# Gradients and inner rows turned by DMA instead of TensorE, PSUM halves kept, large loads held: a four-layer forward and backward

## The chip, the core and the metric

The kernel runs on one core of a Trainium2 chip. Its time is the device time of one execution in microseconds (us); of several executions the median is taken. A profile is a record of one execution of its own. The core has five instruction queues: TensorE (PE; its weight loads are shown as PEld), VectorE (DVE), ScalarE (ACT), GpSimd (POOL) and SyncE (SP). Here SP computes nothing: it issues DMA transfers, in order, and an issue that must wait holds up all that stand behind it. POOL issues some transfers too.

## What is computed

The reference is a forward pass of four residual layers over x [2048, 512], A, B, A, B, and the gradients of its output with respect to x and to five weights. In short:

```
A(x): q, k, v = (x @ wqkv) in 32 heads of 16;  pq, pk = phi(q), phi(k)
      kv = sum_s pk v;  z = sum_s pk;  o = (pq kv) / (pq z + 1e-6);  return o @ wo
B(x): h = sigmoid(x @ w_gate) * (x @ w_up);  return h @ w_down      # inner width 1376
x = x + A(LN(x)); x = x + B(LN(x)); x = x + A(LN(x)); x = x + B(LN(x))
outputs: x, and the gradients for A_x, wqkv, wo, w_gate, w_up, w_down from grad_out
```

Both A layers share their weights, and both B layers theirs, so a weight's gradient is a sum over two layers. Matmul operands are bf16 and sums are f32.

## The kernel before

The 2048 rows stand in 16 tiles of 128 rows, in 4 blocks of 4 tiles (512 rows). The width of 512 is 4 chunks of 128, and the inner width of 1376 is 11 chunks (`NFC`). Layers are called 0 (A), 1 (B), 2 (A), 3 (B). The residual x, later the gradient, stays in SBUF as 16 f32 tiles `k.xs`. The stages in order of time, by the profile of before:

- 0 to 70 us: layer 0 forward, first half (`AFwd.first`: layer norm, keys, sums over all rows).
- 70 to 300 us: its second half (`second`) woven into layer 1 (`b_fwd`, `glu`), then layer 2, whose second half runs beside the start of layer 3.
- 300 to 519 us: layer 3 forward and backward at once (`b_both`, L709). A block makes, for each of 11 chunks, the gate and the up products and the gradient of the inner rows (`g_ps`, `u_ps`, `dhh_ps`), the inner rows `hh` and two gradient factors `dd`. After the second chunk (fc 1) of the next block come `down` (the output rows) and `dh_b` (L796, the gradient to the layer norm, closed by `ln_bwd`, L857).
- 519 to 634 us: layer 2 backward: `a_bwd1` (L970) and `a_bwd2` (L1044).
- 634 to 759 us: layer 1 backward (`b_bwd`, L877).
- 759 to 866 us: layer 0 backward, by the same two functions.
- 866 to 1115 us: the weights' gradients from saved rows (`dw_cols` L1205, `dw_rows` L1227), which need both layers' saved operands with rows on the partitions (`set_t`, `rows_t`).

One gradient is not left to the end. `Fill` (L211) computes layer 3's part of the gradient of w_down as 11 x 16 = 176 single matmuls (`fill_ps`, L236), and `k.fill.step(n)` puts n of them in where TensorE would wait otherwise. Their operand is `hh` of layer 3 with rows on the partitions. Before, `store_hh` (L658) writes `hh` to DRAM as it stands (inner index on the partitions, `sv_hhT`), for layer 3 from POOL's queue, and `Fill.load` (L221) reads it back with a transposing DMA of 16 tiles for each inner chunk (`hf_t`, L224).

`a_grads` (L940) makes a block's gradient ready for the attention's backward: ACT rounds `k.xs` to bf16 (`ga_t`, L947), TensorE turns it in 128x128 pieces (`T_ps`, L951), and ACT copies the turned pieces out of PSUM (`gaT_t`, L953). It is called for block 0 within the stage before, and for the other blocks in halves inside `a_bwd1`. `b_grads` (L957) does the same for layer 1 with a DMA in place of TensorE (L964).

`a_bwd1` loops over 4 blocks and 4 chunks: `dq_ps` (4 matmuls on `gaT_t` and `MT_l`), an ACT copy `dq_sb`, a product `u_t` with the loaded `qp_l`, and `soft` two chunks later (`t_ps`, then DVE, and POOL on the loaded `dqT_t`); a block ends with 16 matmuls into `CT_ps` that need `ga_t` and the loaded `qn_l`. `a_bwd2` first forms small products (`dkvT`, `Wp`, `Nv`), and then for each block `dpk_ps` (16 matmuls on the loaded `haT_l`, drained by DVE into `dkT_t`, L1075, with a factor from the loaded `pkT_l`), and three groups of 16 matmuls into `dh_ps` (L1062, and twice L1123), closed by `ln_bwd`.

The order on each engine is set by a list scheduler that follows the order of the program text and its priorities; `after` and `held` (L184, L191) add an edge by hand, `held` one that a transfer must wait for. Tiles come from pools with a fixed number of buffers: a new tile waits for the last user of the buffer it takes. PSUM has 8 banks. Before, the forward pass takes all 8 from one pool (L342, tag "bank"), and the backward pass opens two new pools of 4 (L814, L815, tags "bank" and "dwbank"). The buffers that the steps name are `h_t` (4; holds `h_t`, `gn_t`, `ga_t`, `qn_l`, `ha_l`), `hT_t` (4), `sh` (2), `set_t` (6) and `hh` (14).

Of the kernel before, what the change touches and what calls it, by code (L numbers as in the profile page):

```python
# [51 lines left out]
class K:  # L52
    pass
# [3 lines left out]
def kernel(  # L57
# [42 lines left out]
    for l in range(4):  # L100
# [11 lines left out]
        else:  # L112
            d["hhT"] = dram.tile([F, S], BF16, name=f"sv_hhT{l}")
            d["ddT"] = dram.tile([2, F, S], BF16, name=f"sv_ddT{l}")
            if l == 3:
                d["g"] = k.g_in
                d["wd"] = dram.tile([F, D], F32, name="sv_wd3")
                d["ddN"] = dram.tile([NBLK, len(SETS), P, 2, NB, D], BF16, name="sv_ddN3")
            else:
                d["g"] = dram.tile([S, D], BF16, name=f"sv_g{l}")  # L120
                d["sd"] = dram.tile([NBLK, NFC, P, 2 * SB], BF16, name=f"sv_sd{l}")
# [4 lines left out]
    k.gns, k.gTs, k.nats = {}, {}, []  # L126

    k.wb = ExitStack()
    forward(k)
# [81 lines left out]
class Fill:  # L211


    def __init__(self, k):
        self.k, self.sv = k, k.sv[3]
        self.g = [k.p_set.tile([P, NB, D], BF16, name="gf_t", tag="set_t") for _ in range(NBLK)]
        for b in range(NBLK):
            k.nc.sync.dma_start(out=self.g[b][:], in_=by_tile(k.g_in, b * NB, NB))
        self.todo = self.run()

    def load(self, fc):  # L221
        t = self.k.p_set.tile([P, NST, P], BF16, name="hf_t", tag="set_t")
        w = min(P, F - fc * P)
        self.k.nc.sync.dma_start_transpose(out=t[:, :, 0:w], in_=self.sv["hhT"][fc * P:fc * P + w, :])  # L224
        return t, w

    def run(self):
        k, nc = self.k, self.k.nc
        ahead = self.load(0)
        for fc in range(NFC):  # L230
            t, w = ahead
            ps = k.ps.tile([P, D], F32, name="fill_ps", tag="bank")
            for st in range(NST):
                if st == 3 and fc + 1 < NFC:
                    ahead = self.load(fc + 1)
                nc.tensor.matmul(ps[0:w, :], lhsT=t[:, st, 0:w], rhs=self.g[st // NB][:, st % NB, :],  # L236
# [12 lines left out]
class LN:  # L249
# [12 lines left out]
    def one(self, st):  # L262
# [5 lines left out]
        if l == 0:  # L268
# [13 lines left out]
            if j % 2 == 0:  # L282
                self.tp = k.ps.tile([P, 2 * NDC, P], BF16, name="T_ps", tag="bank")
# [31 lines left out]
    def turn(self, j):  # L315

        k, nc = self.k, self.k.nc
        tp = k.ps.tile([P, 2 * NDC, P], BF16, name="T_ps", tag="bank")
# [16 lines left out]
def forward(k):  # L335
    nc, tc = k.nc, k.tc
    with ExitStack() as ctx:
# [4 lines left out]
        k.ps = pool("ps_fwd", 8, space=PSUM)  # L342
# [89 lines left out]
class AFwd:  # L432
# [6 lines left out]
    def keys(self, st):  # L439
# [6 lines left out]
        k_ps = k.ps.tile([P, D], F32, name="k_ps", tag="bank")  # L446
# [11 lines left out]
    def first(self, done):  # L458

        k, nc, l, ln = self.k, self.k.nc, self.l, self.ln  # L460
        E_ps = [k.ps.tile([P, D], F32, name="E_ps", tag="bank") for _ in range(NDC)]
        z_ps = k.ps.tile([P, NDC], F32, name="z_ps", tag="bank")
# [30 lines left out]
        self.E_ps, self.z_ps = E_ps, z_ps  # L493

    def query(self, b, d2):
# [5 lines left out]
        for i in range(2):  # L501
            dc = 2 * d2 + i
            q_ps = k.ps.tile([P, SB], F32, name="q_ps", tag="bank")
# [7 lines left out]
    def den(self, b, _=0):  # L511

        k, nc = self.k, self.k.nc
        d_ps = k.ps.tile([P, P], F32, name="den_ps", tag="bank")
# [10 lines left out]
    def share(self, b, d2):  # L525
# [3 lines left out]
        for i in range(2):  # L529
            ps = k.ps.tile([P, SB], F32, name="rd_ps", tag="bank")  # L530
# [19 lines left out]
    def out(self, b, j):  # L550
        k, nxt = self.k, self.nxt
        y_ps = k.ps.tile([P, D], F32, name="y_ps", tag="bank")
# [5 lines left out]
    def products(self, E, kvT):  # L558
# [3 lines left out]
        k2_ps = k.ps.tile([P, NDC, P], F32, name="kv_ps", tag="bank")  # L562
# [5 lines left out]
        for jc in range(NDC):  # L568
            m_ps = k.ps.tile([P, D], F32, name="MT_ps", tag="bank")
# [6 lines left out]
    def second(self, nxt):  # L576
# [19 lines left out]
        kv_ps = k.ps.tile([P, NDC, P], F32, name="kvT_ps", tag="bank")  # L596
# [6 lines left out]
        for c in range(NDC):  # L603
            m_ps = k.ps.tile([P, D], F32, name="M_ps", tag="bank")
# [30 lines left out]
def glu(k, hT, fc, fused=False):  # L635

    nc = k.nc
    g_ps = k.ps.tile([P, SB], F32, name="g_ps", tag="bank")
    mm4(k, g_ps[:], lambda c: k.wg[:, c, FC0[fc]:FC0[fc] + P], lambda c: hT[:, :, c, :])
    u_ps = k.ps.tile([P, SB], F32, name="u_ps", tag="bank")  # L640
# [22 lines left out]
def b_fwd(k, l, ln, nxt):  # L663
# [9 lines left out]
    def down(b):  # L673
        ys = [k.ps.tile([P, D], F32, name="y_ps", tag="bank") for _ in range(NB)]
# [34 lines left out]
def b_both(k, l, ln, ctx):  # L709
# [4 lines left out]
    k.n_t, k.fused = 2, lambda st: True  # L714

    def down(b):
        for j in range(NB):
            st = b * NB + j
            y_ps = k.ps.tile([P, D], F32, name="y_ps", tag="bank")
# [15 lines left out]
    for b in range(NBLK):  # L735
        ln.need(b * NB + NB - 1)
        hhs[b], dds[b] = [], []
        if b == 1:
            k.p_ln, k.p_o, k.p_nat = pool("ln3", 2), pool("o3", 2), pool("nat", 2)
        for fc in range(NFC):  # L740
            hh, dd = glu(k, ln.hT[b], fc)
            ps = k.ps.tile([P, SB], F32, name="dhh_ps", tag="bank")
# [8 lines left out]
            store_hh(k, sv, b, fc, hh, k.st)  # L751
# [7 lines left out]
            if b == NBLK - 1 and fc == 5:  # L759
                k.early = a_grads(k, 0)  # L760
# [4 lines left out]
    dh_b(k, l, b, dds[b], ln.h[b], gns[b])  # L765
    flush_nat(k)
# [17 lines left out]

def flush_nat(k):
# [10 lines left out]
def dh_b(k, l, b, dds, h, up=None):  # L796
    for j in range(NB):
        st = b * NB + j
        dh_ps = k.ps.tile([P, D], F32, name="dh_ps", tag="bank")
# [10 lines left out]
def backward(k):  # L810
    nc, tc = k.nc, k.tc
    with ExitStack() as ctx:
        pool = lambda name, bufs, **kw: ctx.enter_context(tc.tile_pool(name=name, bufs=bufs, **kw))
        k.ps = pool("ps_bwd", 4, space=PSUM)  # L814
        k.ps2 = pool("ps_dw", 4, space=PSUM)  # L815
# [17 lines left out]
        h3, h1 = (load_all(k, sv[l]["h"], k.p_all, "all") for l in (3, 1))  # L833
# [43 lines left out]
def b_bwd(k, l):  # L877
    nc, sv = k.nc, k.sv[l]
    with ExitStack() as ctx:
# [8 lines left out]
        def back(b, fc, dd):  # L888

            if fc == 0:  # L890
                acc[b] = [k.ps2.tile([P, D], F32, name="dh_ps", tag="dwbank") for _ in range(NB)]
# [10 lines left out]
        gTs[0] = k.early  # L902
        for b in range(NBLK):
            if b == NBLK - 1:
                k.early = a_grads(k, 0)
            for f0, nf in FGRP:
# [3 lines left out]
                for fc in range(f0, f0 + nf):  # L910
                    i = fc - f0
                    ps = k.ps.tile([P, SB], F32, name="dhh_ps", tag="bank")
# [12 lines left out]
                    if fc == 3 and b + 1 < NBLK:  # L925
                        grads(b + 1)
        while late:
# [12 lines left out]
def a_grads(k, b, half=None):  # L940
    nc = k.nc
    if half in (None, 0):
        k.ga = (k.p_h.tile([P, NB, D], BF16, name="ga_t", tag="h_t"),
                k.p_hT.tile([P, NB, NDC, P], BF16, name="gaT_t", tag="hT_t"))
    g_t, gT = k.ga
    for j in range(NB) if half is None else range(2 * half, 2 * half + 2):
        nc.scalar.copy(g_t[:, j, :], k.xs[b * NB + j][:])  # L947
        if j % 2 == 0:
            tp = k.ps.tile([P, 2 * NDC, P], BF16, name="T_ps", tag="bank")
        for c in range(NDC):  # L950
            nc.tensor.transpose(tp[:, j % 2 * NDC + c, :], g_t[:, j, c * P:(c + 1) * P], k.ident[:])  # L951
        if j % 2:
            nc.scalar.copy(gT[:, j - 1:j + 1].rearrange("p a c q -> p (a c) q"), tp[:])  # L953
# [319 lines left out]
```

## Time and profile before

| what | value |
|---|---|
| median of 10 runs | 1116.12 us (1113.61 to 1119.72) |
| profiled execution, device time | 1116.56 us |
| its span, first to last instruction | 1114.9 us |
| outside its span | 1.66 us |
| granted TensorE clock | 0.998 |
| PE busy | 1068.8 us (96%), 5529 instructions |
| DVE, ACT, POOL busy | 550.9, 467.7, 303.0 us |
| DMA packets | 377709, 248.12 MB |

The page of a profile lists the busy time of each engine, the load over time in 40 slices, the DMA queues, the chain of work that ended last, and the costliest groups of instructions by line and tile. The view of waits lists for how long an engine stood still before an instruction and what released it. The timeline gives instructions in order: start, length, engine, line, operation, tiles, count, and in brackets the idle time before them. Neighbouring matmuls overlap, so that what one of them takes is read from the distance of two starts, not from its length. The view of windows gives each engine's busy time in a stretch, and the DMA share, a sum over packets divided by 16 engines, which can pass 1.

### The profile page before, as it was taken

How to read it: one execution, taken by the hardware profiler on the slowest of the kernel's cores; microseconds unless marked ns; L12 is line 12 of the kernel's file. 1: busy time of each engine (PE TensorE's matmuls, PEld its weight loads, DVE VectorE, ACT ScalarE, POOL GpSimd, SP SyncE). 2: the span in 40 equal slices, each digit the busy share in tenths (PEclk: the TensorE clock that was granted, in tenths of full speed). 3: DMA queues.
4: the chain of work that ended last, by engine and by line, in shares of the span. 5: the costliest groups of instructions: out<-in, count | busy, mean ns of one | idle time of the engine just before them, and what ended most of it. 6: DMA issues, size and time to landing. Idle time of an engine off the chain costs nothing.

```text
span 1114.9 us, 15529 instructions
## 1 busy us (share of the span) xinstructions
PE 1068.8 (96%) x5529; PEld 508.4 (46%) x5624; DVE 550.9 (49%) x1023; ACT 467.7 (42%) x962; POOL 303.0 (27%) x407
## 2 busy tenths in 40 slices
PE   6989999998889999999999999999999999999998
PEld 3444444444434444444444444444444444465443
DVE  7686866667935445444667535556758200001110
ACT  3476867547735547363434434345435200000010
POOL 5423434203732516140542300002514100011110
PEclk9999999999999999999999999999999999999999
DMA  8978888789995939499995896859985986579993
GB/s 264 266 227 254 251 237 239 209 189 226 289 216 118 247 82 230 98 233 291 282 298 157 239 274 214 234 167 279 348 277 184 262 219 173 131 174 253 260 213 100
DMA packets 377709, 248.12 MB, mean 223 GB/s; under 512 B 288912, under 2 KB 341168, under 8 KB 376864
## 3 DMA queue, kind: packets, MB, share of 16 engines
q1 hardware_dynamic: 362576, 197.73, 71.0%
q0 software_dynamic: 15056, 49.39, 13.0%
q8 instruction: 44, 0.72, 0.3%
q14 instruction: 33, 0.27, 0.1%
HBM read 74.48 MB, written 102.20 MB: 158 GB/s over the span
## 4 chain that ended last, share of the span: by engine, by line
PE 48%; DMA 3%; SPq 3%; DVE 1%; ACT 1%; issue 1%; POOL 0%; ACTq 0%; POOLq 0%; DVEq 0%
PE dw_ps L1217 18%; PE dh_ps L894 7%; PE dh_ps L1123 3%; PE dhh_ps L180 3%; PE dw_ps L1235 3%; PE dh_ps L1062 2%; PE fill_ps L236 2%; PE CT_ps L992 2%; PE dpk_ps L180 2%; PE dq_ps L180 2%; SPq L224 1%; DMA pkT_l<-sv_pkT 1%; SPq L1013 1%; DMA hf_t<-sv_hhT 1%; DMA nat_t<-sd_t 1%
## 5 line engine op out<-in xcount | busy, mean ns | idle before, releaser
L1217 PE MATMUL dw_ps<-set_t,rows_t 128*128 128x512 bf16 (+1 forms) x1008 | 203.6, 362 | 0.8
L1217 PEld LDWEIGHTS <-rows_t 128*128 128x128 bf16 x1024 | 100.1, 98 | 103.6
L654 POOL TENSOR_TENSOR sd_t<-sd_t,hh_t 128x512 bf16<-128x512 bf16 x68 | 83.8, 1233 | 153.8 <-DVE hh_t L649 110.6
L1143 DVE CAST dw_new<-dw_ps 128x512 bf16<-128x512 f32 (+1 forms) x20 | 12.4, 654 | 186.2 <-PE dw_ps L1217 185.0
L1143 ACT CAST dw_new<-dw_ps 128x512 bf16<-128x512 f32 (+1 forms) x20 | 10.5, 561 | 222.2 <-PE dw_ps L1217 201.2
L864 ACT ACTIVATE t_sb<-dh_ps,rstd 128x512 f32<-128x512 f32 x64 | 43.5, 680 | 135.9 <-PE dh_ps L802 98.8
L180 PE MATMUL g_ps<-hT_t,wg 128*128 128x512 bf16 x352 | 90.8, 379 | 4.4 <-ACT hT_t L322 2.3
L180 PE MATMUL u_ps<-hT_t,wu 128*128 128x512 bf16 x352 | 90.3, 379 | 0.6 <-DVE hh_t L649 0.6
L180 PE MATMUL dhh_ps<-gT_t,wdT 128*128 128x512 bf16 x341 | 89.3, 379 | 0.5
L894 PE MATMUL dh_ps<-wuT,dd_t 128*128 128x512 bf16 x173 | 65.6, 379 | 0.2
L649 DVE SCALAR_TENSOR_TENSOR hh_t<-sd_t,u_ps 128x512 bf16<-128x512 bf16 x88 | 59.6, 679 | 10.3 <-ACT sd_t L648 9.4
L894 PE MATMUL dh_ps<-wgT,dd_t 128*128 128x512 bf16 x170 | 64.4, 379 | 0.2
L648 ACT ACTIVATE sd_t<-g_ps,onef 128x512 bf16<-128x512 f32 x88 | 60.4, 690 | 2.8
L728 DVE TENSOR_TENSOR sd_t<-dhh_t,sd_t 128x1024 bf16<-128x1024 bf16 x44 | 30.4, 691 | 62.0 <-POOL sd_t L654 60.7
L1144 POOL DMA_DIRECT2D out_dram<-dw_new x36 | 19.2, 541 | 150.6 <-DVE dw_new L1143 123.5
L917 DVE TENSOR_TENSOR dd_t<-dhh_t,sh_t 128x1024 bf16<-128x1024 bf16 x44 | 29.9, 690 | 58.7 <-ACT dhh_t L915 45.8
L647 ACT ACTIVATE g_ps<-g_ps 128x512 f32<-128x512 f32 x88 | 52.4, 598 | 11.2 <-PE g_ps L180 10.9
L802 PEld LDWEIGHTS <-sd_t 128*128 128x128 bf16 x352 | 34.4, 98 | 45.0 <-issue 3.5
L180 PEld LDWEIGHTS <-wg 128*128 128x128 bf16 x352 | 33.9, 98 | 43.8 <-issue 5.5
L180 PEld LDWEIGHTS <-wu 128*128 128x128 bf16 x352 | 34.4, 98 | 42.3 <-issue 0.9
L894 PEld LDWEIGHTS <-dd_t 128*128 128x128 bf16 x352 | 34.4, 98 | 41.6
L180 PEld LDWEIGHTS <-wdT 128*128 128x128 bf16 x352 | 34.4, 98 | 41.5 <-issue 0.3
(174 smaller groups left out, 1883.0 us busy)
## 6 DMA issues: line engine op xcount, KB each, us to landing
sv_sd<-sd_t SPq DMA_DIRECT2D x44, 256.0 KB, 3.0
sv_ddT<-dd_t SPq DMA_DIRECT2D x40, 256.0 KB, 4.7
sv_h<-h_t POOLq DMA_DIRECT2D x16, 512.0 KB, 5.3
sv_qr<-pe_t POOLq DMA_DIRECT2D x16, 512.0 KB, 4.7
sh_t<-sv_sd SPq DMA_DIRECT2D x8, 1024.0 KB, 6.9
rows_t<-sv_h SPq DMA_DIRECT2D x16, 512.0 KB, 7.2
sv_ddN<-nat_t SPq DMA_DIRECT2D x6, 1024.0 KB, 4.9
set_t<-sv_ddN SPq DMA_DIRECT2D x12, 512.0 KB, 5.6
```

The source lines that it names most:

```text
L180: i = k.nc.tensor.matmul(out, lhsT=lhs(c), rhs=rhs(c), start=(c == 0), stop=(c == n - 1))
L647: nc.scalar.activation(g_ps[:], g_ps[:], ACT.Tanh, scale=-0.5)
L648: nc.scalar.activation(sd[:, 0, :], g_ps[:], ACT.Identity, bias=k.onef[:], scale=-1.0)
L649: nc.vector.scalar_tensor_tensor(hh[:], sd[:, 0, :], 0.5, u_ps[:], ALU.mult, ALU.mult)
L654: nc.gpsimd.tensor_tensor(sd[:, 1, :], sd[:, 1, :], hh[:], ALU.mult)
L728: k.last_mul = nc.vector.tensor_tensor(dd, dhh[:].unsqueeze(1).to_broadcast([P, 2, SB]), dd, ALU.mult)
L802: k.nc.tensor.matmul(dh_ps[:], lhsT=dds[fc][:, a, rows(j)], rhs=(k.wuT, k.wgT)[a][:, fc, :], start=(i == 0), stop=(i == 2 * NFC - 1))
L864: nc.scalar.activation(t_sb[:], dh_ps, ACT.Identity, scale=rstd, accum_out=c1[:])
L894: nc.tensor.matmul(acc[b][j][:], lhsT=dd[:, a, rows(j)], rhs=(k.wuT, k.wgT)[a][:, fc, :], start=(fc == 0 and a == 0), stop=(fc == NFC - 1 ...
L1123: nc.tensor.matmul(dh[j][:], lhsT=lhs(j, c), rhs=rhs(c), start=False, stop=stop and c == NDC - 1)
L1217: k.nc.tensor.matmul(ps[ic][:, 0:w], lhsT=h_m[:, ic * P:(ic + 1) * P], rhs=t_m, start=(m == 0), stop=(m == n - 1))
L1235: k.nc.tensor.matmul(p[0:r, :], lhsT=t[:, f:f + r], rhs=g_t, start=(i == 0 and st == 0), stop=(i == len(srcs) - 1 and st == NST - 1))
```

## The change

It has these parts:

1. `a_grads` turns by DMA: ACT still rounds, but the transposes on TensorE and the ACT copies out of PSUM go; SP issues a transposing DMA for every two tiles, SBUF to SBUF. It is called for whole blocks: blocks 0 and 1 in the stage before (`b_both` chunks 5 and 7 of the last block; `b_bwd` chunks 0 and 5 of the last block), blocks 2 and 3 in `a_bwd1`, in blocks 0 and 2.
2. Layer 3's `hh` of blocks 1 to 3 is turned in SBUF by SP (`turn_hh`) and stored with rows on the partitions (`sv_hhN`) by SP, one chunk later; POOL's stores of them go. `Fill.load` reads 12 tiles plainly and turns 4 (block 0).
3. One PSUM pool with both tags for all stages. In the forward pass and layer 3 `bank` takes the halves in turn (`spread_banks`); while the sums of `AFwd.first` stand in one half, and in the backward pass, it takes the other.
4. Loads in the attention's backward are moved or held: `qp_l` and `dqT_t` of a block until the second `dq_sb` of the block before; `qn_l` at its own block; layer 2's turned weights `woT`, `wqkvT` to chunk 1 of block 1, behind those loads, `wdT` into `a_bwd2`; the rows `h3`, `h1` for the weights' gradients until `dkT_t` of block 2 and of block 3 of layer 0.
5. `a_bwd2`'s first block adds the values' part before the keys' matmuls, and half of the `Nv` copies go to DVE. The 12 fill matmuls at the head of `a_bwd1` go; layer 2's first block takes 0, 6, 6, 6 instead of 2, 2, 2, 2. `w_t` has 3 buffers, `ab_o` of layer 0 has 3.

```diff
 class K:
-    pass
+    spread_banks, n_bank = True, 0
+    def bank(self, shape, dtype, name):
+        self.n_bank += 1
+        if self.spread_banks and self.n_bank % 2:
+            return self.bank2(shape, dtype, name)
+        return self.ps.tile(shape, dtype, name=name, tag="bank")
+    def bank2(self, shape, dtype, name):
+        return self.ps.tile(shape, dtype, name=name, tag="dwbank")
...
     def load(self, fc):
         t = self.k.p_set.tile([P, NST, P], BF16, name="hf_t", tag="set_t")
-        w = min(P, F - fc * P)
-        self.k.nc.sync.dma_start_transpose(out=t[:, :, 0:w], in_=self.sv["hhT"][fc * P:fc * P + w, :])
+        p0 = FDUP if fc == NFC - 1 else 0
+        self.k.nc.sync.dma_start(out=t[:, NB:NST, :], in_=self.sv["hhN"][fc, :, NB:NST, :])
+        self.k.nc.sync.dma_start_transpose(out=t[:, 0:NB, p0:P], in_=self.sv["hhT"][fc * P:fc * P + P - p0, 0:SB])
...
-            store_hh(k, sv, b, fc, hh, k.st)
+            if b:
+                turn_hh(k, sv, b, fc, hh)
+            else:
+                store_hh(k, sv, b, fc, hh, k.st)
...
+def turn_hh(k, sv, b, fc, hh):
+    t = k.p_hn.tile([P, NB, P], BF16, name="hn_t")
+    k.nc.sync.dma_start_transpose(out=t[:], in_=hh[:])
+    if k.hns:
+        dst, old = k.hns.pop()
+        k.nc.sync.dma_start(out=dst, in_=old)
+    k.hns.append((sv["hhN"][fc, :, b * NB:(b + 1) * NB, :], t[:]))
...
-            if b == NBLK - 1 and fc == 5:
-                k.early = a_grads(k, 0)
+            if b == NBLK - 1 and fc in (5, 7):
+                k.early.append(a_grads(k, len(k.early)))
...
-def a_grads(k, b, half=None):
+def a_grads(k, b):
...
         nc.scalar.copy(g_t[:, j, :], k.xs[b * NB + j][:])
-        if j % 2 == 0:
-            tp = k.ps.tile([P, 2 * NDC, P], BF16, name="T_ps", tag="bank")
-        for c in range(NDC):
-            nc.tensor.transpose(tp[:, j % 2 * NDC + c, :], g_t[:, j, c * P:(c + 1) * P], k.ident[:])
         if j % 2:
-            nc.scalar.copy(gT[:, j - 1:j + 1].rearrange("p a c q -> p (a c) q"), tp[:])
+            nc.sync.dma_start_transpose(out=gT[:, j - 1:j + 1].rearrange("p a c q -> p (a c) q"),
+                                        in_=g_t[:, j - 1:j + 1, :].rearrange("p a d -> p (a d)"))
...
     loads(0)
-    k.fill.step(12)
...
-            k.fill.step(2)
+            k.fill.step(2 if b or l == 0 else 6 if dc else 0)
...
-            if dc in (0, 2) and b + 1 < NBLK:
-                g = a_grads(k, b + 1, dc // 2)
-                if dc:
-                    gs.append(g)
-                    loads(b + 1)
+            if dc == 0 and b in (0, 2):
+                gs.append(a_grads(k, 2 + b // 2))
+            if dc == 1 and b + 1 < NBLK:
+                loads(b + 1)
+                if b == 1 and l == 2:
+                    held(k, k.mark, nc.sync.dma_start_transpose(out=k.woT[:], in_=k.w_in["wo"]),
+                         nc.sync.dma_start_transpose(out=k.wqkvT[:], in_=k.w_in["wqkv"]))
...
-        nc.scalar.copy(Nv[:, c, :], ps[:])
+        (nc.vector.tensor_copy if c % 2 else nc.scalar.copy)(Nv[:, c, :], ps[:])
+    values(0, dh)
     dks = [keys(0)]
...
-        h3, h1 = (load_all(k, sv[l]["h"], k.p_all, "all") for l in (3, 1))
+        h3, h1 = (load_all(k, sv[l]["h"], k.p_all, "all", k.marks[b]) for l, b in ((3, 2), (1, 3)))
```

In the instruction lists, TensorE's loses 128 transposes and gains nothing. SP issues 604 transfers instead of 511 (33 `hn_t` turns, 33 `sv_hhN` stores, 11 more `hf_t` loads, 16 `gaT_t` turns), and POOL 147 instead of 180.

## The prediction

> **What bounds the kernel.** I read the page's busy shares and slices first, then TensorE's own waits, and then its timeline around each of them.
>
> ```profile
> PE 1068.8 (96%) x5529; PEld 508.4 (46%) x5624; DVE 550.9 (49%) x1023; ACT 467.7 (42%) x962; POOL 303.0 (27%) x407
> ...
> PE   6989999998889999999999999999999999999998
> ...
> DMA  8978888789995939499995896859985986579993
> ...
> DMA packets 377709, 248.12 MB, mean 223 GB/s; under 512 B 288912, under 2 KB 341168, under 8 KB 376864
> ```
>
> TensorE is the bound in nearly every slice; the DMA engines come second, with slices of 9. Three packets in four are under 512 B: turned data. So TensorE work that goes is worth its full time, as long as the DMAs that replace it aren't late.
>
> ```profile
> PE fill_ps L236 <- DVE dkT_t L1075: 2.4, 1, 2.4
> ...
> PE dpk_ps L180 <- DMA haT_l<-sv_hT: 1.5, 1, 1.5
> ...
> PE t_ps L997 <- DVE u_t L1001: 1.0, 1, 1.0
> PE fill_ps L236 <- ACT t_sb L864: 0.9, 1, 0.9
> ...
> PE fill_ps L236 <- DMA hf_t<-sv_hhT: 0.6, 1, 0.6
> ```
>
> These are TensorE's waits in the backward stages that the change touches (total, times, longest): 6.4 us. The larger waits of the list lie before 333 us, where next to nothing changes.
>
> **Part 1, the transposes.** The timeline of TensorE in layer 3:
>
> ```profile
> 475.15 1.03 PE L180 MATMUL dhh_ps<-gT_t,wdT 128*128 128x512 bf16 x4
> 476.01 1.06 PE L951 MATMUL T_ps<-ident,ga_t 128*128 128x128 bf16 x16
> 476.90 1.03 PE L180 MATMUL g_ps<-hT_t,wg 128*128 128x512 bf16 x4
> ```
>
> From start to start, 16 transposes take 476.90 - 476.01 = 0.89 us, 56 ns each (a single record shows 219 ns, but neighbours overlap). In the attention, 8 take 0.45 (523.53 to 523.98). The view of L951 counts 128, so 128 x 0.056 = **-7.2 us**, within 7.0 to 7.4. None of it lay beside an idle TensorE: 2.7 us in each `a_bwd1`, 0.9 in layer 3, 0.9 in `b_bwd`.
>
> The Trainium skill ("TensorE: Matmul & The Clock Gate", Part 4: PE-mode transpose) gives about 275 ns for a 128x128 transpose within a kernel. That would make it 128 x 0.275 = 35 us. The distance of the starts decides against it here.
>
> ACT loses 16 copies `gaT_t` of 1.01 us. But in layer 3 the 4 roundings `ga_t` of 0.62 us become 8: 4.96 us against 4 x 0.62 + 2 x 1.01 = 4.50. In 466 to 490 us ACT is busy 23.6 of 24; 0.5 us more is hidden by free PSUM banks and by 490 to 519, where it is busy 4.2 of 29. I take 0, at most +0.5.
>
> The price is on SP and the DMAs: 16 turns of 128x1024. The nearest row is the same shape from SBUF, `nat_t`:
>
> ```profile
> L775 SPq DMA_TRANSPOSE nat_t<-sd_t x33: 1231/1563/3247, 333.0 to 496.6; - x33
> ```
>
> Minimum, median and maximum of an issue are in ns; they land 4.5 us after it. Blocks 0 and 1 are turned over 25 us before their use, so they are hidden. Blocks 2 and 3 are priced with part 4.
>
> **Part 2, the inner rows.** The turned total is equal: 33 x 512 columns now, 11 x 1536 fewer in `hf_t`. What changes is the place.
>
> ```profile
> 440.00:490.00 50.00, 49.74 (x240) 23.16 (x244) 23.14 (x38) 26.68 (x53) 17.05 (x21) 1.00 0.60 136
> 490.00:519.00 29.00, 28.57 (x130) 12.62 (x130) 11.26 (x19) 4.24 (x13) 4.55 (x6) 1.00 1.08 300
> 519.00:567.00 48.00, 45.84 (x253) 22.51 (x259) 31.97 (x67) 25.08 (x43) 21.50 (x21) 1.00 1.10 274
> ```
>
> The last three columns are clock, DMA share and GB/s. Turns move from stretches of share 1.08 and 1.10 to one of 0.60. SP adds for each chunk a half-size turn (half of 1.23 to 1.56, an estimate of 0.6 to 0.8 us) and a store (0.40, the median of such SP stores at L660) beside `nat_t`: 2.2 to 2.8 us a chunk. TensorE needs 12 x 0.216 = 2.6 in the dense chunks, and 58.9 / 11 = 5.4 us over a whole block. SP may fall some microseconds behind in the dense part and catches up while `down` and `dh_b` run (29 us). I take 0. Without that cover, see the second rival.
>
> POOL loses 33 issues of 0.58 us; it waited 110.6 us for `hh_t`, so this is worth 0.
>
> `fill_ps` no longer waits for `hf_t`: **-0.6**.
>
> **Part 3, PSUM.** With the halves in turn there are still 8 banks in turn, so layer 3 sees what it saw: waits for a bank there come to 2.5 us now (`g_ps` 1.1 and 0.8, `u_ps` 0.6). Halves are less free when tiles are released out of order. Ends: -1 and +2.5; I take +0.3. At 519 us the first tile of the new pool waited 0.9 us for ACT; now `dq_ps` comes first and takes a half whose bank is long drained: **-0.9**. Next late would be `MT_l`. It was issued at 508.9 and lands after 6.6, at 515.5, against 518.8; now it stands ahead of the four `gf_t` (5.0 us of SP). So it is covered.
>
> **Part 4, the loads.** SP in the layer 2 backward, before:
>
> ```profile
> 508.94 1.06 SPq L973 DMA_DIRECT2D MT_l<-sv_MT  x1
> 510.05 8.82 SPq L224 DMA_TRANSPOSE hf_t<-sv_hhT  x2
> 518.91 2.17 SPq L1012 DMA_TRANSPOSE woT<-in_A_wo_dram  x1
> 521.13 6.83 SPq L1013 DMA_TRANSPOSE wqkvT<-in_A_wqkv_dram  x1
> ```
>
> Block by block, `a_bwd1` on TensorE, with 0.865 for 4 matmuls, 0.216 for one: block 0 has 3.5 (`dq`) + 18 x 0.216 + 0.4 + 3.45 (`CT`) = 11.3, from 518.8 to 530.1; blocks 1 and 2 take 9.5 each, so block 3 starts at 549.1.
> - `qn_l` of block 0 waits for a buffer `h_t` until the last `ln_bwd` (DVE is done at 521.9). It lands 3.9 to 6.6 later, at 526 to 528.5. `CT_ps` wants it at 526.6. Ends 0 and +2; I take +0.5. Behind it in SP's queue wait `dqT_t`, the turns of block 2 and the loads of block 1. These are wanted from 531 on.
> - `woT` and `wqkvT` now go out after about 532, 9.0 us of issue, and the turns of block 3 stand behind them: issued 541 to 544.5. They land after 4 to 10 us (`nat_t`'s 4.5 to `wqkvT`'s 10.0), at 548 to 554, and are wanted at 549.1. Ends 0 and +5; I take +1.5.
> - `wdT` leaves this stage (9.0 us of issue, 12.3 to landing) and goes ahead of the last `pkT_l` in `a_bwd2`. Ends 0 and +2; I take +0.3.
> - `t_ps` waited 1.0 for DVE, which stood behind POOL's wait for `dqT_t`. `w_t` has a third buffer, but `dqT_t` comes later too: **-0.5**, ends 0 and -1.0.
> - In layer 0 the eight `rows_t` loads (14.1 us of SP between 768.7 and 783.4) leave `a_bwd1`, and `haT_l` of block 2 is no longer behind two `set_t` turns (12.1 us of SP at 811): **-1.2** of the 1.5. `h3` is then issued from about 828 and wanted at 853; `h1` comes after it, wanted 13.8 later. I take 0 for the lateness; the third rival prices it.
>
> **Part 5.** The values' part first needs `Nv` at once: 4 copies of 0.6 on two engines against 0.86 of matmuls leave a wait of 0.4 in layer 2 (ends 0 and 1.5; fills cover it in layer 0): +0.4. The 2.4 us wait of a new `fill_ps` comes from DVE, which stood 6.6 us at `pkT_l`. That tile's buffer is freed no earlier than before, but its landing (7.3 us) falls in a lighter queue. The fill count again needs a new tile there. So **-1.0**, ends 0 and -2.4.
>
> **Sum.** -7.2 - 0.6 - 0.9 - 0.5 - 1.2 - 1.0 = -11.4, and +0.3 + 0.5 + 1.5 + 0.3 + 0.4 = +3.0: -8.4. The profiled execution took 1116.56, 0.4 above the median, so 1108.2 against it, and 1107.7 against 1116.12. Against the median, all terms at their good ends: -7.4 - 0.6 - 0.9 - 1.0 - 1.0 - 1.5 - 2.4 = -14.8, 1101.3. All at their bad ends: -7.0 - 0.6 - 0.9 - 1.2 and + 0.5 + 2.5 + 2 + 5 + 2 + 1.5 = +3.8 would be 1119.9; all of them together is unlikely.
>
> **Rivals.**
> 1. *The DMAs bound layer 2's `a_bwd1`.* For it: share 1.10 there, and every load of blocks 1 to 3 is now issued late and behind 9 us of turned weights. Against it: `wdT` and most of `hf_t` leave the stage. Priced at +5 for the turns of block 3, +2 for `qn_l`, and no gain from the three waits by DVE and DMA: -8.4 + 3.5 + 1.5 + 2.7 = -0.7 at worst, half of it on average: 1111 to 1116.
> 2. *Slower: SP falls behind in layer 3.* A store waits for a landing; if each waits the full 4.5 us of a turn less the 2.6 of a chunk, a chunk costs SP 2.8 + 1.9 = 4.7, and 33 make 155 us. With the waits for `gn_t` (29.4 us in two) that is 184 of the 177 us of three blocks, and the head of the attention is late by what doesn't fit. It decides only when `MT_l` is issued more than 3.3 us later than now (8 if its move ahead of `gf_t` holds), and the time is above 1116 only when TensorE waits over 8 us at 519: 1117 to 1125. Against it: turns were issued one after another with 2.4 us between them, so landings overlap.
> 3. *What is gained is given back at the weights' gradients.* `h3` and three `set_t` arrive late since they are held and wait for `fill`'s buffers: 4 to 8 us: 1112 to 1116. Against it: 25 us between issue and use, and a stretch of share 0.75.
> 4. *All waits go*: 1101 to 1104.
>
> **Chances.** The forecast (1104 to 1111) 0.55, rival 1 0.17, rival 2 0.08, rival 3 0.08, rival 4 0.12. About 0.2% (2.2 us) is what a measurement here can tell from no change. Faster: 0.55 + 0.12 + 0.10 + 0.04 = 0.81; the same: 0.05 + 0.04 = 0.09; slower: 0.08 + 0.02 = 0.10. The range from 1101 to 1115 leaves out rival 2 and the upper ends of rivals 1 and 3.
>
> **What would show it.** Right: PE's count lower by 128; no `T_ps<-ident,ga_t`; the waits on `t_sb` at the head of layer 2's attention, on `hf_t` and on `haT_l` gone; the stage from 866 us as long as now (249 us). Wrong: a wait of `dq_ps` or `CT_ps` on a DMA of over 3 us (rival 1); `MT_l` issued after 515 (rival 2); `dw_ps` waiting for `rows_t` or `set_t` (rival 3). A forward pass longer before 333 us would say that the halves of PSUM cost more than I took.

## The result and the profile after

The changed kernel takes 1125.88 us (median of 15 runs, 1121.78 to 1133.03) against 1116.61 for the kernel before, measured beside it (52 runs): a ratio of 1.0088 with a 95% interval of 1.0071 to 1.0105. It is slower by 0.9%, where the prediction had 0.8% faster. The profiled execution has a span of 1125.5 us and a granted clock (the share of TensorE's full clock that it was given) of 0.992; before, these were 1114.9 and 0.998.

The page of the changed kernel, the lines that answer to those of before:

```profile
PE 1070.6 (95%) x5402; PEld 503.7 (45%) x5496; DVE 552.7 (49%) x1027; ACT 452.1 (40%) x942; POOL 286.6 (25%) x374
...
PE   6989999998899999998798999999999999999998
...
DMA  8988888779996979699999696777989996579994
...
DMA packets 400798, 256.84 MB, mean 228 GB/s; under 512 B 307424, under 2 KB 363904, under 8 KB 399952
```

TensorE has 127 instructions fewer (a record can be missing), yet is busy 1.8 us longer: some matmuls must have run slower. The slices have new dents at the 19th, 20th and 22nd (506 to 563 and 591 to 619 us), and the DMAs carry 8.7 MB more. TensorE's waits from 500 us on (total, times, longest):

```profile
PE dpk_ps L192 <- DVE dkT_t L1104: 6.1, 3, 5.5
PE dq_ps L192 <- DMA gaT_t<-ga_t: 4.8, 1, 4.8
PE dq_ps L192 <- issue: 3.7, 1, 3.7
PE fill_ps L250 <- DMA hf_t<-sv_hhT: 2.3, 1, 2.3
PE CT_ps L1015 <- DMA qn_l<-sv_qn: 1.7, 3, 1.1
PE dq_ps L192 <- ACT dq_sb L1039: 1.3, 3, 0.5
```

The waits that the change was to take away are gone (`t_sb`, `haT_l`, `u_t` but for 0.3 us). Four longer ones stand in their place. "issue" at 518.4 hides a DMA: `dq_ps` needs `MT_l`, which was issued at 511.45 and landed 6.9 us later, at 518.4. SP's queue shows what each transfer stands behind:

```profile
536.54 0.45 SPq L1008 DMA_DIRECT2D dqT_t<-sv_qr  x1
537.03 9.24 SPq L1051 DMA_TRANSPOSE woT<-in_A_wo_dram  x1
546.31 6.22 SPq L1052 DMA_TRANSPOSE wqkvT<-in_A_wqkv_dram  x1
552.63 3.61 SPq L975 DMA_TRANSPOSE gaT_t<-ga_t  x2
...
589.53 13.66 SPq L1144 DMA_TRANSPOSE wdT<-in_B_w_down_dram  x1
603.30 1.35 SPq L1074 DMA_DIRECT2D pkT_l<-sv_pkT  x1
```

`gaT_t` of block 3, wanted at 553.6, is issued at 552.6, after 15.5 us of turned weights. The last `pkT_l` is issued at 603.3, after 13.7 us of `wdT`; DVE then stood still until 610.1, and `dkT_t`, which `dpk_ps` waits for, came late:

```profile
610.12 0.69 DVE L1097 TENSOR_SCALAR dph_t<-pkT_l 128x2048 bf16<-128x2048 bf16 x1 [9.81 <-DMA pkT_l<-sv_pkT]
```

The three turned weights hold SP for 29.1 us in sum, against 18.0 before (2.17, 6.83, 8.99).

The rest is in the view of windows. These are stretches around the waits (length, PE busy and count, PEld, DVE, ACT, POOL, granted clock, DMA share, GB/s):

```profile
514.57:517.98 3.41, 0.23 (x2) 0.00 (x0) 1.45 (x3) 0.98 (x3) 0.00 (x0) 1.00 1.03 307
517.98:521.39 3.41, 2.94 (x7) 1.02 (x8) 0.42 (x2) 0.59 (x1) 0.00 (x0) 0.50 1.14 254
...
555.53:558.94 3.41, 0.56 (x3) 0.32 (x4) 0.00 (x0) 0.00 (x0) 0.00 (x0) 1.00 1.13 257
558.94:562.35 3.41, 3.41 (x10) 1.22 (x8) 0.86 (x2) 0.59 (x1) 0.00 (x0) 0.50 0.90 318
...
651.10:654.51 3.41, 1.14 (x6) 0.33 (x5) 1.37 (x3) 2.04 (x5) 1.25 (x1) 1.00 1.13 240
654.51:657.92 3.41, 3.19 (x9) 1.30 (x9) 0.69 (x1) 0.80 (x2) 1.32 (x2) 0.50 1.07 401
```

A stretch in which TensorE mostly stood still is followed by one with the clock at 0.50: from 558.94 there are 10 matmuls in 3.41 us of work; at full clock 16 to 18 stand there. After the wait of 5.5 us there are two (613.55 to 620.38). Of these 17 us the busy part, 3.19 + 3.41 + 4.9 + 2.94 = 14.4, ran at half speed, so about 7.2 us were lost to the clock. In the kernel before only one such stretch stands in the trace, in its first 20 us.

The marks of the stages, from the timelines of TensorE, give the account:

| stretch | before | after | difference |
|---|---|---|---|
| start to the end of the last `dh_ps` of layer 3 | 518.8 | 514.8 | -4.0 |
| to the first `dhh_ps` of layer 1 (layer 2 backward) | 115.5 | 129.6 | +14.1 |
| to the last `dh_ps` of layer 1 (layer 1 backward) | 125.1 | 128.2 | +3.1 |
| to the first `dw_ps` (layer 0 backward) | 106.5 | 103.7 | -2.8 |
| to the end | 249.0 | 249.2 | +0.2 |

Layer 2: waits of 3.65 + 4.77 + 5.50 and 2.3 of small ones, 5.6 for the clock, less the transposes (2.7) and the old waits (1.0 + 2.4 + 0.9): +14.8 against +14.1 measured. Layer 1: 2.27 + 1.6 for the clock, less 0.9: +3.0 against 3.1. Of the -4.0 at the start, 2.9 are a wait for `wgT` at 331 us (3.22 before, 0.29 now); over the traces of all versions it lay anywhere between nothing and 3.8 us, so this is no gain of the change. 0.9 are transposes; the forward pass up to 327 us was 1.3 longer, within the spread of the traces (326.3 to 328.2), and the rest of layer 3 shorter by about as much.

### The profile page after: what moved, and what is told of

It reads as the page before. It is cut to its first block, busy times and chain, and to the rows that moved or that the text cites. A ratio compares the mean times of both kernels' runs of the same rounds, so it can differ in the third digit from the quotient of the medians.

```text
span 1125.5 us, 15371 instructions
## 1 busy us (share of the span) xinstructions
PE 1070.6 (95%) x5402; PEld 503.7 (45%) x5496; DVE 552.7 (49%) x1027; ACT 452.1 (40%) x942; POOL 286.6 (25%) x374
## 4 chain that ended last, share of the span: by engine, by line
PE 48%; DVE 3%; DMA 2%; SPq 2%; issue 1%; ACT 1%; POOL 0%; DVEq 0%; ACTq 0%; POOLq 0%
PE dw_ps L1247 18%; PE dh_ps L922 7%; PE dh_ps L1092 4%; PE dw_ps L1265 3%; PE dhh_ps L192 3%; PE dh_ps L1083 2%; PE fill_ps L250 2%; PE dpk_ps L192 2%; PE dh_ps L831 2%; PE dq_ps L192 2%; PE CT_ps L1015 2%; DMA qn_l<-sv_qn 1%; DVE t_sb L897 1%; DVE junk L896 1%; SPq L1051 1%
## 5 line engine op out<-in xcount | busy, mean ns | idle before, releaser
L1023 POOL TENSOR_TENSOR dqT_t<-w_t,dqT_t 128x512 bf16<-128x512 bf16 x32 | 37.8, 1192 | 64.1 <-DMA dqT_t<-sv_qr 38.3
L941 ACT ACTIVATE dhh_t<-dhh_ps 128x512 bf16<-128x512 f32 x44 | 26.3, 597 | 68.4 <-PE dhh_ps L192 62.7
```

The lines of the kernel that those rows point to most:

```text
L1023: nc.gpsimd.tensor_tensor(dqT[:, dc, :], w_t[:], dqT[:, dc, :], ALU.mult)
```

## The experiments

Theory: a few transfers are late, each behind turned weights or turns in SP's queue, and each costs its wait and a stretch at half clock. Rival: the transfers of the stage are too many as a whole, and order doesn't matter. Times are medians. The kernel before, measured again beside each group of runs, took 1116.6 to 1118.2.

### One stall at a time

e1 moves `wdT` behind the last `pkT_l`:

```diff
-        if b == 1 and not final:
+        if b == 2 and not final:
             held(k, k.marks[b], nc.sync.dma_start_transpose(out=k.wdT[:], in_=k.w_in["wd"]))
```

> The changed kernel, with wdT issued one block later in layer 2's second half (b == 2 in place of b == 1), so that the last pkT_l goes out ahead of it. Theory (the loss is made of single stalls behind SP's queue, each followed by a stretch at half clock): the 5.50 us wait of dpk_ps for dkT_t at 615.5 goes, and with it the clock of 0.5 from 615.5 to 620.4, worth 2.4: 1125.9 - 7.9 = 1118, within 1116.5 to 1120. Rival (the DMA engines as a whole are late in this stage, whatever stands first in the queue): dkT_t or the first dhh_ps of the next stage waits 4 us or more in its place, and the time is 1123 to 1127.

1126.4 us. The wait for `dkT_t` went, and `dhh_ps` of layer 1 waited 5.93 us instead: `wdT`, now at 604, stands ahead of the turns `gT_t`, and ACT waits for those, by its view of waits:

```profile
ACT g_t L985 <- DMA gT_t<-g_t: 17.2, 3, 9.0
```

Besides, the wait for `gaT_t`, which lies ahead of the edit, was 10.02 us in this execution (`wqkvT` held SP for 13.59). The rival's numbers held.

e2 moves `woT` and `wqkvT` behind the turns of block 3 (`b == 2` in place of `b == 1`).

> The changed kernel, with woT and wqkvT issued behind the turns and loads of block 3 (b == 2 in place of b == 1). Theory: the 4.77 us wait of dq_ps for gaT_t at 558.4 goes, and the half clock up to 562.4, worth 1.7: 1125.9 - 6.5 = 1119.4, within 1117.5 to 1122; woT is issued about 549 and lands ahead of the first use at 572. Rival (DMA engines late as a whole): dkvT_ps or the first dh_ps waits 3 us or more for woT or wqkvT, and the time is 1123 to 1127.

1128.0 us: `gaT_t` came in time, but `dh_ps` waited 5.08 us for `wqkvT`. The rival again, 1 us above its range.

e3 takes the last block's inner rows from SP:

```diff
-            if b:
+            if 0 < b < NBLK - 1:
                 turn_hh(k, sv, b, fc, hh)
...
-        self.k.nc.sync.dma_start(out=t[:, NB:NST, :], in_=self.sv["hhN"][fc, :, NB:NST, :])
+        self.k.nc.sync.dma_start(out=t[:, NB:NST - NB, :], in_=self.sv["hhN"][fc, :, NB:NST - NB, :])
```

and `Fill.load` turns blocks 0 and 3 from `sv_hhT`.

> The changed kernel, with the inner rows of layer 3's last block stored untouched by POOL as before, and turned when they are read (two turned loads and one plain one for each hf_t). SP loses 11 turns and 11 stores in the last dense part. Theory (MT_l at 511.45 is late only because SP stands behind its own turns): MT_l is issued at 509 or before, the wait of 3.65 us at 518.4 falls under 1 us and the half clock after it goes: 1125.9 - 3 - 1.5 = 1121.4, within 1119.5 to 1123. Rival (MT_l and what follows wait for the DMA engines or for memory that the last products hold): MT_l goes out within 1 us of 511.4 all the same and the time stays within 1124 to 1127.

1121.9 us: as the theory had it. `MT_l` went out at 501.38 instead of 511.45, and no wait stood at 518. So SP's own turns made it late. `gaT_t` (5.39) and `dkT_t` (4.74) still waited.

> The three edits together. Theory: they are separate stalls and add up: 1125.9 - 7.9 - 6.5 - 4.5 = 1107, within 1104 to 1110, so below the kernel before (1116.6) by about 0.9%, which is what the prediction's sum had without the three stalls. Rival (total DMA load): a stall removed comes back at the next transfer, less than half of the 19 us is got back, and the time is above 1115.

1120.6 us; the sum of 19 us failed. Two waits are left, both behind turned weights, which hold SP for 26.9 us (the second by way of ACT and `gT_t`, as in e1):

```profile
PE dh_ps L1085 <- DMA wqkvT<-in_A_wqkv_dram: 7.2, 1, 7.2
PE dhh_ps L192 <- ACT dhh_t L943: 4.7, 1, 4.7
```

### One part undone

u1 gives the turn of the gradients back to TensorE.

> The changed kernel with part 1 undone: the attention's gradients are turned on TensorE and copied out by ACT again, at the new places. 128 transposes come back (+7.2), 16 turned transfers leave SP. Theory after the first four runs (SP's queue between 500 and 610 us holds more turned transfers than it can issue in time, whichever stands first): the wait for gaT_t goes (4.8 and 1.7 of half clock) but woT, wqkvT and wdT still stand where they do, MT_l too: 1123 to 1129, so part 1 costs about what it saves. Rival (part 1 alone makes the loss): under 1119.

1131.9 us, 6.0 above the changed kernel by the medians, about 4 by the two ratios to the kernel before (1.0121 and 1.0088). So part 1 saves something, in the order of the 7.2 of the prediction; more can't be read from this run, since its waits are others too. Waits of 3.18 at 522, 3.98 in block 3 and 5.30 for `dkT_t` are still there, so the late turned weights hurt without part 1, too.

u2 gives all inner rows back to POOL.

> The changed kernel with part 2 undone: the inner rows of layer 3 stored by POOL as they stand, hf_t turned as it is read (16 tiles in one transfer). SP loses 33 turns and 33 stores in layer 3, and gets longer turned loads in layer 2 (4 of them before 580 us, some 24 us of SP in the kernel before against 7 now). Theory (queue of SP): MT_l goes out near 503 and its wait goes (-5), but the longer hf_t loads add to the queue in layer 2 and gaT_t or wdT waits grow by about as much: 1121 to 1128. Rival (the turns of layer 3 are the whole cause): under 1118.

1126.5 us (12 runs, 1117.7 to 1134.5), as expected: part 2 in sum shows no worth. `MT_l` is early (504.65), but `gaT_t` waits 5.73, `qn_l` 2.33, `hf_t` 3.06.

u3 opens separate PSUM pools again.

> The changed kernel with part 3 undone: 8 banks in one pool in the forward pass, two new pools of 4 in the backward pass. Theory (part 3 is worth little here): within 1.5 us of the changed kernel, 1124 to 1127.5, with MT_l as the wait at 518 either way. Rival (halves in turn cost banks in the forward pass and layer 3): 3 us or more below it, and the stretch before 515 us shorter.

1127.1 us: part 3 has no share that shows.

u4 undoes part 4 in `a_bwd1`, and `wdT` goes back there:

> The changed kernel with part 4 undone in layer 2 and layer 0's first half: qp_l, dqT_t and qn_l loaded without being held, woT and wqkvT at the start of block 1 and unheld, wdT at block 3 as before; the holds on h3 and h1 stay. Theory (the turned weights were moved 13 to 38 us later, into the stretch where the turns of block 3 and the last pkT_l are due): the waits of 4.8 for gaT_t and 5.5 for dkT_t go, with 1.7 and 2.4 of half clock; the wait for MT_l stays: 1112 to 1117. Rival (the total of the transfers, whatever their order, as e1 and e2 seem to say): 1121 to 1128.

1128.8 us. The two named waits went, and one of 14.2 came:

```profile
PE CT_ps L1015 <- DMA qn_l<-sv_qn: 16.2, 2, 14.2
```

`qn_l` of block 0 takes a buffer `h_t`. There are four, and with the early `a_grads` of block 1 the last one is free only after the last `ln_bwd`; by then `woT` and `wqkvT` (12.5 us of SP) are ahead. So part 1 needs part 4. b1 shows the same from the other side, the kernel before with part 1 alone:

> The kernel before with part 1 alone: a_grads by DMA for whole blocks, called where the changed kernel calls it; all else as before. Theory: 7.2 us of transposes go, but ga_t of block 1 now holds a fourth buffer of h_t early, so that qn_l of block 0 must wait for the last ln_bwd and goes out behind woT and wqkvT (as in u4e3): CT_ps waits 7 to 9 us with some 2 us of half clock, 1117.4 - 7.2 + 10 = 1120, within 1116 to 1124. Rival (turning by DMA is a clean gain, and the loss is all in the other parts): 1108 to 1111.

1135.9 us, far above the 1120 expected. The wait for `qn_l` came (2.89 and 4.86), but the largest is one that I had not named, in layer 0. `haT_l` of block 2 stands behind three turned `set_t` for the weights' gradients there, 9.14 + 15.53 us of SP:

```profile
PE dpk_ps L180 <- DMA haT_l<-sv_hT: 11.7, 1, 11.7
```

### Two undone, and the order mended

u4 and e3 together:

> The two edits together: loads of the attention's backward as in the kernel before, and the last block's inner rows stored by POOL. Theory (late turned weights, and SP's lag at 511): both go, 1107 to 1113, under the kernel before. Rival (total of the transfers): 1117 to 1124, no better than the last block by POOL alone (1121.9).

1116.5 us, between theory and rival: the loss is gone, one wait of 8.70 for `qn_l` of block 0 remains. x1 puts that load ahead of the weights:

```diff
+            if dc == 1 and b == 0 and l == 2:
+                after(k, nc.sync.dma_start_transpose(out=k.woT[:], in_=k.w_in["wo"]), qn0)
+                after(k, nc.sync.dma_start_transpose(out=k.wqkvT[:], in_=k.w_in["wqkv"]), qn0)
```

> The kernel of u4e3 with one change of order: qn_l of block 0 goes out first, then the turns of block 2, then woT and wqkvT, all in block 0 (an edge by hand puts the weights behind qn_l). Theory (each loss has one named transfer that stands behind turned weights in SP's queue): u4e3 has one wait left in the stage, 8.70 us of CT_ps for qn_l, with about 2.1 us of half clock after it; both go: 1116.5 - 10.8 = 1105.7, within 1103 to 1109, 1% below the kernel before. Rival (total of the transfers in the stage): the wait comes back at the next due transfer (dqT_t of block 1, gaT_t of block 3 or haT_l), 4 us or more, and the time is 1112 to 1118.

1116.2 us. The wait moved to `qn_l` of block 1 (7.32 us). The rival's number, at a transfer that it had not named.

> x1 with the next hf_t loaded at the first of the 16 fill matmuls instead of the fourth (st == 0 in place of 3). Every kernel since the change waits 1.8 to 3.1 us for hf_t near 645 to 657, with a half clock stretch behind it in most. Theory (two loads in place of one, and 3.2 us between the issue and the use): the wait falls by 0.6 to 1.5 and the half clock (up to 1.7) may go: 1 to 3 us below x1. Rival (the buffer of hf_t is freed only then, and SP is late anyway): same as x1 within 1 us.

1113.3 us, ratio to before 0.9946 (0.9926 to 0.9967). The wait for `hf_t` is gone. This is the fastest complete version, 0.5% below the kernel before.

> x1 with wdT put back where the changed kernel has it (second half of the attention's backward, block 1, ahead of the last pkT_l). Theory: with everything else mended, this one move costs the wait of dpk_ps for dkT_t, 4.7 to 6.3 us in the runs so far, and 2 to 2.5 of half clock: 7 to 9 us above x1. Rival (it only matters because the queue is late already): under 3 us above x1.

1122.0 us, 5.8 above x1, between the theory's 7 to 9 and the rival's 3: the wait for `dkT_t` is back with 6.35 us. So the same transfers in another order cost 5.8 us: order does matter here.

x4 puts `wqkvT` behind `qn_l` of block 1, x5 is x4 with the last block turned by SP again.

> x2 with wqkvT put behind qn_l of block 1, so that the order is qn_l of block 0, turns of block 2, woT, qn_l of block 1, wqkvT; layer 0's loads as in the changed kernel. Theory (one named transfer behind turned weights for each loss): the 7.2 us wait of CT_ps for qn_l at 539 goes with 2 us of half clock, and layer 0's wait of 3.2 for qn_l at 773 with 0.2 to 1.5: 1113.3 - 9.2 - 3 = 1101, within 1098 to 1106. Rival (total of the transfers): gaT_t of block 3, haT_l or wqkvT waits 4 us or more in its place: 1108 to 1114.

> x4, but with the inner rows of the last block turned by SP as in the changed kernel (33 turns and 33 stores by SP in place of 22 and 22). Theory (SP's lag at the end of layer 3): MT_l goes out near 511 again, dq_ps waits 3 to 4 us at 518 and gf_t about 1, with 1.5 to 3 of half clock, and what follows is 5 to 8 us later in SP's queue: 5 to 12 us above x4. Rival (MT_l's lateness only takes the time by which layer 3 became shorter): at most 3 us above x4.

x4: 1116.8 us, not 1101, and above the rival's range, too. The wait moved on, to `qn_l` of block 2, 7.22 us at 547; the issue of `wqkvT` took 12.18 us here. TensorE's waits:

```profile
PE CT_ps L1023 <- DMA qn_l<-sv_qn: 11.5, 3, 7.2
PE dq_ps L192 <- ACT dq_sb L1049: 3.1, 4, 2.5
```

x5: 1122.3, 5.5 above x4 (waits of 4.00 at 518 and 4.82 at 532), at the low end of the theory. So three orders (u4e3, x1 and x4) each left one wait of 7 to 9 us. Is that the sum of all transfers, or the turning of the weights?

### The same bytes, not turned

```diff
-nc.sync.dma_start_transpose(out=k.woT[:], in_=k.w_in["wo"])
+nc.sync.dma_start(out=k.woT[:], in_=k.w_in["wo"].rearrange("(c p) j -> p c j", p=P))
```

and likewise for `wqkvT` and `wdT` (only the call is shown; the edges around it stay).

> x4 with woT, wqkvT and wdT loaded as they stand, without turning (equal bytes, rows of 1 to 3 KB; wdT's place is filled from w_gate, which has its shape). It leaves out the turning of the weights in layer 2 and 1, so what comes after is computed from wrong weights; the instructions of the compute engines are the same. Theory (it is the turned weights that hold SP and the DMA engines up for 6 to 12 us each): the 7.2 us wait for qn_l of block 2 goes with 2 us of half clock, and the issues of the three fall from 20 us in sum to under 4: 1116.8 - 9 = 1108, within 1104 to 1110. Rival (all transfers of the stage together, turned or not): a wait of 5 us or more stays in the stage and the time is 1113 to 1117.

1108.2 us, 8.6 below x4. That is the time that the prediction had, but by leaving the turning out. The issues of the three take 0.57, 0.43 and 0.38 us, and TensorE's waits are:

```profile
PE CT_ps L1023 <- DMA qn_l<-sv_qn: 4.3, 4, 2.3
PE dq_ps L192 <- ACT dq_sb L1049: 3.3, 3, 2.9
```

The two long ones lie in layer 0; none over 1 us is left in layer 2, although the DMAs move more there: from 500 to 580 us 332 GB/s against 295 in x4, at a share of 1.07 against 1.12. So a share above 1 doesn't say that no more bytes go through.

> The changed kernel with the same three loads untouched by turning (the same part of the work is left out). Theory: the waits of 4.8 us for gaT_t and 5.5 for dkT_t go, with 1.7 and 2.4 of half clock, while MT_l's 3.7 at 518 and hf_t's 2.3 at 654 stay: 1125.9 - 14.4 = 1111.5, within 1109 to 1115. Rival (all transfers together): 1120 or more.

1116.0 us, 9.9 below the changed kernel, 1 us above the theory's range: `dkT_t`'s wait is gone, `gaT_t`'s is down to 2.14, `MT_l`'s (3.78) and `hf_t`'s (2.02) stand as expected. The turning of three weights at these places is thus worth as much as the whole loss (9.3). The kernel before turns them too and was not run without, so how much of this it pays as well stays open.

### The clock by itself

> A measurement by itself; it computes nothing of the reference and stores zeros. TensorE makes bursts of 60 to 66 matmuls of 128x512, with gaps between them of about 1 to 5 us (a chain of 0 to 17 small ACT copies), three times through, then bursts of 4, 8 and 16 matmuls with the shortest gap; SP turns 128x512 and 128x1024 from SBUF one at a time and 12 at once, then woT, wqkvT and wdT. Theory on the clock (the share of TensorE's time in fixed stretches of 3.41 us decides, as the records of the runs so far stand on one grid): gaps under 1.7 us never halve it, gaps over 3.4 nearly always, gaps between by where they fall, and the bursts of 4 stay at half clock though no gap reaches 1.7. Rival (the length of one gap decides, over about 3 us): gaps of 2 to 3 us never halve it. On the turns: an issue takes 1.2 us on an idle queue for both sizes, and over 12 at once the larger size takes up to twice as long as the smaller.

The halved stretches start on one grid of 3.413 us. Three gaps (2.14 us; 2.63; 3.85), as windows on that grid:

```profile
117.93:121.34 3.41, 1.27 (x7) 0.51 (x6) 0.00 (x0) 1.86 (x7) 0.00 (x0) 1.00 0.00 0
121.34:124.76 3.42, 3.42 (x10) 1.22 (x8) 0.00 (x0) 0.00 (x0) 0.00 (x0) 0.50 0.00 0
...
786.94:790.36 3.42, 1.40 (x7) 0.53 (x6) 0.00 (x0) 1.73 (x9) 0.00 (x0) 1.00 0.00 0
790.36:793.77 3.41, 2.80 (x7) 1.01 (x7) 0.00 (x0) 0.56 (x1) 0.00 (x0) 0.50 0.00 0
...
885.93:889.34 3.41, 1.43 (x7) 0.56 (x6) 0.00 (x0) 1.70 (x8) 0.00 (x0) 1.00 0.00 0
889.34:892.76 3.42, 1.55 (x8) 0.72 (x8) 0.00 (x0) 1.65 (x6) 0.00 (x0) 1.00 0.00 0
```

The longest of the three didn't halve the clock: it was split into 1.98 and 1.87 us. Over all windows, up to 1.98 us of idle time (0.58) left the clock full, and from 2.02 us (0.59) on the next window was at half. So the share in a window decides, not the length of the gap. Its limits were wrong, though: the bursts of 4, idle for 0.73 of every 1.75 us (0.42), stayed at full clock. Back to full it went after windows with at most 0.61 us of idle time (0.18); 0.92 (0.27) kept it at half. At the start of the other kernels' traces these limits don't hold: in the kernel before, windows with 3.41 and 2.80 us of idle time (0.13 to 6.95 us) left the clock full, and one with 1.86 (10.37 to 13.78) halved it.

On the turns: small and large ones, queued together, took 1.3 to 3.6 us each, so the run doesn't separate the sizes. The three weights, the last in the queue, took 2.27, 6.70 and 5.85 us: 14.8 in sum with only turns under way. At the head of the same queue, with stores by POOL beside them, `woT` and `wqkvT` took 1.36 and 11.27.

## Why the prediction was wrong

- **The transposes, -7.2**: right in kind; all 128 are gone, and u1 is 4 to 6 us slower, with other waits.
- **"`MT_l` ... is covered", -0.9 at 519**: failed, and the step is SP's pace in layer 3, for which it took 0. The size behind that is the "half-size turn (... an estimate of 0.6 to 0.8 us)", which isn't half:

```profile
L807 SPq DMA_TRANSPOSE hn_t<-hh_t x33: 1188/1258/3747, 332.1 to 503.2; - x33
L794 SPq DMA_TRANSPOSE nat_t<-sd_t x33: 1231/1232/3168, 334.2 to 507.7; - x33
```

  Half the columns cost SP the same 1.2 us. With the store a chunk took 1.26 + 0.53 + 1.23 = 3.0 beside the 2.6 of TensorE. So `MT_l`, though ahead of the `gf_t` now, went out 2.5 us later than before. Cost: 3.65 us, 1.5 of clock. This was rival 2's mechanism at a lower threshold than the 3.3 us it was given. That margin was misread, too: 6.6 us to landing is the middle of two `MT_l`, and layer 2's took 8.1 (to 517.0), which leaves 1.8 to 518.8. And `dh_b` ended at 514.8 now, mostly by the chance of `wgT`. But that didn't make the wait: in e2, where `wgT` took 3.75 us, `dh_b` ended at 518.7, `MT_l` went out at 514.65, and `dq_ps` waited 3.44.
- **`gaT_t` of block 3, +1.5 (ends 0 and +5)**: the mechanism named, the size not: 4.77 and 1.7 of clock, in other runs up to 10. The step took 9.0 us for the issue of `woT` and `wqkvT`, from before; at the new place it was 15.5. The sign that the text named for rival 1 showed here: a wait on a DMA of over 3 us.
- **`wdT` ahead of the last `pkT_l`, +0.3 (ends 0 and +2)**: the largest miss; 5.50 and 2.4 of clock (x3: 5.8 us by itself). It counted 9.0 us for an issue that took 13.7, and did not look at who stands behind DVE's wait.
- **`hf_t`, -0.6**: the old wait went, but one of 2.27 came in layer 1, since a tile now needs two loads and the second went out 3.3 us ahead of its use. x2 removes it.
- **The 2.4 us wait of `fill_ps`, -1.0; `haT_l`, -1.2; `t_ps`, -0.5**: gone as said, the first wholly. **`Nv`, +0.4, and PSUM, +0.3**: neither shows (u3). **`qn_l` of block 0, +0.5**: 0.31. **The last stage**: as long as before (249.2).
- **No term for the clock.** Each long wait cost 1.5 to 2.5 us more than its length, about 7 in sum. The kernel before has such a wait too, 3.22 us at 332, but its idle time lies in two windows (views of before):

```profile
327.78:331.20 3.42, 1.73 (x9) 0.69 (x7) 1.44 (x3) 0.00 (x0) 2.48 (x4) 1.00 1.28 305
331.20:334.61 3.41, 1.83 (x8) 0.87 (x9) 2.93 (x5) 0.00 (x0) 1.77 (x4) 1.00 0.96 263
```

- **The range**: its bad ends added up to +3.8, 1119.9, which the text called unlikely. Three terms, that of `MT_l` among them, had no bad end at all. Those of `gaT_t` and `wdT` shared one cause, turned weights that held SP for longer than at their old places (29.1 us against 18.0), and came together; rival 1 summed them to -0.7 "at worst" without the clock and without `wdT`.

Why did a turned weight hold SP for 2 us at one time and for 10 at another? A DMA share above 1.0 doesn't tell: `woT` took 2.17 us before at a share of 1.19 and 9.24 after at 1.07. What went out just ahead of it does, in all 17 traces of whole kernels with a turned `woT`: right behind a turned transfer it took 1.95 to 3.76 us (8 traces), right behind a plain load that was still under way 5.55 to 10.16 (9). In x1 and then in e3:

```profile
518.35 3.33 SPq L977 DMA_TRANSPOSE gaT_t<-ga_t  x2
521.73 2.03 SPq L1055 DMA_TRANSPOSE woT<-in_A_wo_dram  x1
...
528.75 0.43 SPq L1010 DMA_DIRECT2D dqT_t<-sv_qr  x1
529.23 6.73 SPq L1053 DMA_TRANSPOSE woT<-in_A_wo_dram  x1
```

It isn't the place in time: at 533.6 in x5, behind turns of `ga_t`, it took 2.91 us, and at 533.8 in u2, behind `dqT_t`, 10.16. Before, `woT` stood behind two turned `hf_t`; the change put it behind `qp_l` and `dqT_t`. This is an observation over the traces: no run changed that neighbour alone, `wqkvT` and `wdT` don't sort as cleanly (`wqkvT` took 13.59 behind `woT` in e1), and the reason stays open. So is whether the turned weights do their harm by holding SP or by what they load on the DMA engines, since no run issued them from another queue. A place for them in layer 3 wasn't tried.

## What to carry to other kernels

A transfer that turns data is priced twice: the bytes, and the time for which its issue blocks everything behind it on that queue, which for one and the same transfer lay between 2 and 10 us here; list what stands behind it and when each is due, and try to move the blocker rather than the victim; e1 and e2 show that the blocker can then hit the next one. When stalls share one blocker, add their bad ends instead of treating them as independent. Work taken from the bounding engine brings every transfer's due time forward, so test each landing against the new schedule.

## What the runs showed of the hardware

- TensorE's granted clock is decided in fixed windows of 3.413 us: from about 15 us after the start on, over 2.0 us of idle time in one window (0.58) halves the next one, and it stays at half until a window with little idle time (0.18 was enough, 0.27 not). The Trainium skill ("TensorE: Matmul & The Clock Gate", Part 1: The HAM clock gate) also has a free-running window of 3413 ns, but puts the cold state after at least one idle window and sums up as no idle gaps over about 3.4 us. The measurement decides: a gap of 2.14 us halved the clock, one of 3.85 us didn't.
- The grid has another phase in each trace, so the same wait can cost more in one execution and less in another. In 120 executions of the kernel before, a mean clock of 0.997 or more went with a median of 1116.4 us (86 of them, 1113.0 to 1123.2), one of 0.995 or less with 1121.6 (26, 1119.5 to 1127.3).
- Issue of a turn from SBUF: 1.19 us at least for 128x512, 1.23 for 128x1024. Issue of `wqkvT` (512x1536): 6.2 to 13.6 us turned, 0.4 to 0.5 plain. Issue of `woT` (512x512): 2.0 to 3.8 us right behind a turned transfer, 5.6 to 10.2 right behind a plain load.
